# Another list of orders and engines for 1571 operations of an attention and feed-forward kernel

## The chip, the cores and the metric

The kernel runs on one core of a Trainium2 chip. The metric is the time of one execution on the device in microseconds (us); of the runs before the change the median is 259.77 us (three runs, 259.72 to 259.9). TensorE (PE in the rows) multiplies matrices, VectorE (DVE), ScalarE (ACT) and GpSimd (POOL) do the elementwise work, SyncE (SP) only starts transfers. GpSimd and ScalarE start some transfers as well.

## The reference

A Nystrom attention with 32 landmarks over 8 batches of 8 heads, 576 rows and 64 columns, then a feed-forward layer with a residual on its output (8 x 576 rows of 512):

```python
q_lm = q.reshape(B, H, m, S // m, D).mean(axis=3)          # m = 32 landmarks
k_lm = k.reshape(B, H, m, S // m, D).mean(axis=3)
A = sm(q, k_lm); Bm = sm(q_lm, k_lm); C = sm(q_lm, k)      # sm: softmax of a b^T / sqrt(D)
Z = Bm.transpose(0, 1, 3, 2) / (norm1(Bm) * norminf(Bm) + 1e-06)
for _ in range(6):
    Z = 2 * Z - Z @ Bm @ Z
x = A @ Z @ C @ v                                          # heads side by side: (8, 576, 512)
xn = (x - mean(x)) / sqrt(var(x) + 1e-06) * g_ln
out = x + relu(xn @ w_ch1) @ w_ch2                         # w_ch1 512 x 2048, w_ch2 2048 x 512
```

`norm1` and `norminf` stand for the two matrix norms; the sums and means are over each head or row.

## The kernel before, in words

**The stages of one batch.** q and k of a batch are loaded and cast to 16 bits (`nat_q`, `nat_k`; two units of four heads each). Sums over the 18 rows of a segment give the landmarks (for batch 1 the products `psl_q` and `psl_k`, with `pairs16`). A product of landmarks (`psb`), its softmax, and six steps of the iteration give Z: a step is a few matmuls on tiles of 32 rows into the tile `it` (`it<-st`), after which VectorE makes the next state `st` from it (`next_`, L210). The steps alternate between the two engines, and another step can't begin before that state is there. Batch 1 alone forms set 1, batches 2 and 3 set 2, 4 and 5 set 3, 6 and 7 set 4; batch 0 has its own code (`def_batch0`, L531). C v (`product`, `cv`) and Z are multiplied into `zt` (TensorE's `pszt`, then a copy) and into `zc`, from which VectorE makes `zsum` and `zcbd`. The numerator of A is `ea`, scaled by its row sums (`psd`, a logarithm and an exponential on ScalarE, `norm` on GpSimd or VectorE).

**The feed-forward layer.** W1 comes in eight loads through a staging buffer (`stg`, six buffers that q, k and v of batch 0 use first) and is scaled by g_ln in sixteen operations (`scale_w1`, L352 to L357) on GpSimd, ScalarE or VectorE. W2 comes in four loads on GpSimd's queue, straight into place. Because x = ea^T zcbd, the first layer is taken as ea^T (zt W1): four products `psm` per batch, on tiles of 64 rows and 32 columns, then a copy `m` (for batches 0 and 1 with the correction `less` for the mean, made of `psf`, a sum of four matmuls over W1), and then 16 chunks `psh`, each followed by a relu on ScalarE (L203) or VectorE (L1068) into `hT`. The second layer is `pso` = hT^T W2 by blocks of 128 rows (batches 0 and 1, in pairs of matmuls) or, from batch 2 on, seven products of half-size blocks (`ps7a`, `ps7c`, `ps7e`) with sums of parts of hT (`hmix`) and of W2 (`mix`) in front of them. The rows x themselves are `psy`; `done` and `add7` on VectorE add the second layer to them, and two stores per block (`store`, on SyncE, ScalarE or GpSimd) write 128 KB each.

**What sets the order.** Every operation is registered with its name, the engines that may do it, the buffers that it uses and a function (`op`, L158). The table `ORDER` (from L19) lists all 1571 of them by number, with a letter for the engine: P TensorE, D VectorE, A ScalarE, G GpSimd, S SyncE. The loop at the end of the program goes through it:

```python
    for n, e in order:
        emit(n, e)
```

`emit` (L174) takes a buffer for a name at its first use, in the order of the list, and gives it back behind the last use; `keep` (L188) fixes that each engine works through its instructions in that order. So the list sets three things: the order on each engine, the engine of each operation that may go to several, and which buffer a load has to wait for. There are two PSUM buffers of two banks (`p2`) and four of one bank (`bank`). At the start 80 matmuls on zeros (`idle`, the operations `warm`) keep TensorE busy while the first loads are under way; these too have their places in the list.

## Time and profile before

| | |
|---|---|
| median of the runs | 259.77 us (259.72 to 259.9) |
| the profiled execution | 260.21 us |
| its span | 258.5 us |
| TensorE busy | 249.3 us, 96% of the span, 3499 matmuls |
| VectorE busy | 212.1 us, 82%, 472 instructions |
| ScalarE busy | 164.0 us, 63%, 304 instructions |
| GpSimd busy | 177.6 us, 69%, 180 instructions |
| moved by DMA | 36.32 MB, mean 140 GB/s |

The span reaches from the first to the last instruction that the profiler recorded; the execution's time is 1.71 us longer than it. A busy share is taken over the whole span. A row of the timeline gives the start and the length of a run of equal instructions on one engine in us, the engine, the line of the program, the operation, the tile written and the tiles read, the shape, how many instructions there are (x8), and in brackets how long the engine stood idle before it and what ended that. TensorE's rows overlap by the time that a matmul needs to drain, so the time between two starts says what a group costs, not its length. "L193" is the helper through which every matmul goes, so groups are told apart by their tiles.

### The profile page before, as it was taken

The numbers are of one execution on the slowest core, as the hardware profiler recorded it, in microseconds if no ns is written. First come the engines' busy times: TensorE is split into PE (matmuls) and PEld (weight loads), VectorE is DVE, ScalarE is ACT, GpSimd is POOL, SyncE is SP. The second block draws the span as 40 slices with busy tenths as digits, with TensorE's granted clock in tenths as the row PEclk, the third lists the DMA queues.
The fourth block names the chain that finished last, engine by engine and source line by source line (L and its number), as shares of the span: only waits on it lengthen the run. The fifth ranks groups of instructions, "written<-read, shape, count | busy, mean of one in ns | idle before, by whom it ended". The sixth has DMA issues, their size and how long they took to land.

```text
span 258.5 us, 8352 instructions
## 1 busy us (share of the span) xinstructions
PE 249.3 (96%) x3499; PEld 178.4 (69%) x3499; DVE 212.1 (82%) x472; ACT 164.0 (63%) x304; POOL 177.6 (69%) x180
## 2 busy tenths in 40 slices
PE   7689999999999999999999999999999999999994
PEld 7566565555654457777776787777867787788882
DVE  1669899999999989996998879887537999878761
ACT  1588886737766899778756996878766246544000
POOL 8324899689893789699999996782068505966600
PEclk9999999999999999999999999999999999999998
DMA  6999999999749275949814832400130100500356
GB/s 236 364 281 341 365 207 202 207 230 258 230 121 161 44 160 80 207 100 279 144 21 111 235 96 63 114 16 3 41 85 0 44 20 3 122 22 14 90 120 185
DMA packets 23278, 36.32 MB, mean 140 GB/s; under 512 B 2117, under 2 KB 11593, under 8 KB 23241
## 3 DMA queue, kind: packets, MB, share of 16 engines
q1 hardware_dynamic: 12376, 23.34, 29.9%
q0 software_dynamic: 9504, 10.36, 25.3%
q10 hardware_dynamic: 1360, 2.10, 3.2%
q8 instruction: 27, 0.44, 0.7%
q14 instruction: 11, 0.08, 0.1%
HBM read 36.70 MB, written 9.44 MB: 178 GB/s over the span
## 4 chain that ended last, share of the span: by engine, by line
PE 88%; DMA 6%; ACT 2%; DVE 1%; issue 0%; POOL 0%; ACTq 0%; POOLq 0%
PE psh L193 24%; PE ps7a L193 16%; PE pso L193 15%; PE ps7c L193 8%; DMA nat_q<-in_q_dram 5%; PE ps7e L193 4%; PE psm L193 4%; PE psy L193 3%; PE it L193 3%; PE psec L193 2%; PE pscv L193 2%; DMA stg_k<-in_k_dram 2%; PE psd L193 1%; PE psea L193 1%; PE psf L193 1%; PE pso_74a L193 1%
## 5 line engine op out<-in xcount | busy, mean ns | idle before, releaser
L203 ACT ACTIVATE hT<-psh 128x576 f16<-128x576 f32 x106 | 65.8, 650 | 30.4 <-PE psh L193 28.6
L193 PEld LDWEIGHTS <-hT 128*128 128x128 f16 x688 | 64.4, 98 | 23.3 <-issue 3.7
L193 PE MATMUL psh<-ea,m 128*128 128x288 f16 x512 | 78.3, 287 | 0.1
L193 PEld LDWEIGHTS <-m 128*128 128x128 f16 x512 | 48.8, 98 | 15.7 <-issue 1.3
L193 PE MATMUL pso<-w,hT 128*128 128x512 f16 x176 | 45.7, 380 | 0.1
L207 POOL TENSOR_TENSOR mix<-hT 128x1024 f16<-128x1024 f16 x8 | 17.0, 2128 | 27.4 <-ACT hT L203 27.4
L210 DVE SCALAR_TENSOR_TENSOR x<-ps7a,rstd,x 128x256 f32<-128x256 f32 x48 | 21.3, 476 | 6.2 <-PE ps7a L193 4.4
L193 PE MATMUL ps7a<-mix,hT 128*128 128x256 f16 x192 | 25.6, 273 | 0.0
L1068 DVE TENSOR_SCALAR hT<-psh 128x576 f16<-128x576 f32 x22 | 16.4, 753 | 10.1 <-PE psh L193 9.9
L997 DVE BATCH_NORM_STATS2 six<-x 128x6 f32<-128x512 f32 x36 | 24.2, 673 | 0.0
L207 POOL TENSOR_TENSOR ea<-ea,lns 128x576 f16<-128x576 f16 (+1 forms) x14 | 17.7, 1261 | 8.0 <-ACT lns L203 4.3
L200 ACT CAST m<-psm 128x512 f16<-128x512 f32 (+1 forms) x25 | 19.1, 792 | 4.5 <-PE psm L193 3.4
L200 ACT COPY x<-psy 128x512 f32<-128x512 f32 (+1 forms) x29 | 16.8, 587 | 7.7 <-PE psy L193 7.3
L193 PEld LDWEIGHTS <-mix 128*128 128x128 f16 x192 | 18.3, 98 | 4.3 <-issue 1.5
L207 POOL TENSOR_TENSOR mix<-mix,hT 128x1024 f16<-128x1024 f16 x8 | 17.0, 2127 | 6.2 <-DVE mix L207 5.8
L207 POOL TENSOR_TENSOR hT<-hT 128x1024 f16<-128x1024 f16 x9 | 19.1, 2123 | 0.2
L207 POOL TENSOR_TENSOR hT<-hT,mix 128x1024 f16<-128x1024 f16 x7 | 15.1, 2169 | 4.4 <-PE ps7e L193 2.5
L214 DVE TENSOR_REDUCE part<-xT_k 128x32 f16<-128x576 f16 x24 | 17.1, 736 | 0.0
L207 POOL TENSOR_TENSOR asum_q<-asum_q 128x256 f32<-128x256 f32 (+1 forms) x24 | 15.1, 629 | 1.5
L203 ACT ACTIVATE ec<-psec 128x256 f16<-128x256 f32 (+1 forms) x42 | 12.4, 431 | 5.3 <-PE psec L193 5.3
L193 PE MATMUL psy<-zcbd,ea 128*128 128x256 f16 x80 | 14.8, 273 | 0.2 <-ACT x L200 0.2
L357 POOL TENSOR_SCALAR w<-w1s,g_sb 128x512 f16<-128x512 f32 x12 | 8.2, 693 | 9.4 <-DMA w1s<-in_moe_w_ch_dram 5.5
(174 smaller groups left out, 473.1 us busy)
## 6 DMA issues: line engine op xcount, KB each, us to landing
out_dram<-x SPq DMA_DIRECT2D x55, 128.0 KB, 2.6
stg_v<-in_v_dram SPq DMA_DIRECT2D x10, 576.0 KB, 5.9
w1s<-in_moe_w_ch_dram SPq DMA_DIRECT2D x8, 512.0 KB, 11.6
nat_q<-in_q_dram POOLq DMA_DIRECT2D x7, 576.0 KB, 8.3
nat_k<-in_k_dram POOLq DMA_DIRECT2D x7, 576.0 KB, 8.2
w<-in_moe_w_ch_dram POOLq DMA_DIRECT2D x4, 512.0 KB, 9.0
out_dram<-x ACTq DMA_DIRECT2D x15, 128.0 KB, 2.4
stg_v<-in_v_dram SPq DMA_DIRECT2D x6, 288.0 KB, 4.3
```

The lines of the kernel that those rows point to most:

```text
L193: keep(nc.tensor.matmul(o, l, r, start=start, stop=stop, tile_position=(rb, cb), skip_group_check=(skip or cb != 0)))
L200: keep(nc.scalar.copy(o, i) if e == "A" else ENGINES[e].tensor_copy(out=o, in_=i))
L203: keep(nc.scalar.activation(*args, **kw))
L207: keep(ENGINES[e].tensor_tensor(out=o, in0=a, in1=b, op=f))
L210: keep(ENGINES[e].scalar_tensor_tensor(out=o, in0=a, scalar=s, in1=b, op0=f0, op1=f1))
L214: keep(nc.vector.tensor_reduce(out=o, in_=i, axis=axis, op=f))
L357: keep(ENGINES[e].tensor_scalar(out=o, in0=src, scalar1=g_sb[:, kk:kk + 1], scalar2=0.0, op0=ALU.mult, op1=ALU.add))
L997: keep(nc.vector.bn_stats(out=T(f"six_{j}")[:], in_=T(f"x_{j}")[:]))
L1068: keep(nc.vector.tensor_scalar(out=o, in0=T(psh)[:, :, 0:HS], scalar1=0.0, scalar2=None, op0=ALU.max))
```

## The change

Only the table `ORDER` is exchanged; no other line differs. Both lists hold the same 1571 operations, and TensorE has 622 of them in both. Its first rows:

```diff
-0G 20P 23P 4S 12P 14P 24P 17P 11P 2S 1S 3S 6S 7S 10P 21P 28G 38P 25A 26D 34P 39D 40P 29P 30A 31P 27D
...
+0G 21P 4S 18P 12P 23P 22P 14P 2S 24P 20P 17P 11P 10P 1S 25D 3S 13P 28G 40P 38P 39D 6S 26A 34P 27D 7S
...
```

Of operations that may go to several engines these change theirs: of the relus 18 go from VectorE to ScalarE and 6 back; of the stores 19 go from SyncE to ScalarE, 10 from ScalarE to SyncE and 2 to GpSimd; of the sums of parts of hT (`hmix`) 11 go from VectorE to GpSimd and 10 back; of the copies `m` 8 go from ScalarE to VectorE and 6 back; of the copies `x` 7 go from ScalarE to VectorE and 5 back; of the operations `norm` 4 go from VectorE to GpSimd and 3 back; a few casts and scalings move too. By operations, VectorE has 398 before and 388 now, ScalarE 312 and 331, GpSimd 153 and 154, SyncE 86 and 76.

**Batch 0's iteration on TensorE.** `it` holds the products of its steps, a new `st` marks a new step; `psl_q` reads q of batch 1, `psf` reads W1, `psd` belongs to `ea`, and `pszt` is the product behind the last step. LDWEIGHTS loads the operand that stays in the array. Before, from the fourth step on:

```order
L193 MATMUL it_366<-st_578 32x64
...
L193 MATMUL it_366<-st_593 32x64
...
L193 MATMUL psd_603<-ea_572,bones_75 128x288
...
L193 MATMUL psl_q_608<-nat_q_427,pairs16_68 128x128
...
L193 MATMUL idle_622<-zeros_63 128x128
...
L193 MATMUL it_366<-st_620 32x32
...
L193 MATMUL pszt_643<-st_641,cv_618 32x32
...
L193 MATMUL psf_677<-w1_16_78,lesser_74 128x512
```

Now, from the second step on:

```order
L193 MATMUL it_407<-st_556 32x64
...
L193 MATMUL it_407<-st_575 32x64
...
L193 MATMUL psl_q_592<-nat_q_473,pairs16_68 128x128
...
L193 MATMUL it_407<-st_590 32x64
...
L193 MATMUL psf_617<-w1_16_78,lesser_74 128x512
...
L193 MATMUL it_407<-st_613 32x64
...
L193 MATMUL psd_630<-ea_579,bones_75 128x288
...
L193 MATMUL it_407<-st_634 32x32
...
L193 MATMUL psf_617<-w1_16_78,lesser_74 128x512
...
L193 MATMUL pszt_652<-st_644,cv_577 32x32
```

The first nine `psl_q` matmuls stood behind the fifth step and `psd`, with fillers behind them; now they stand behind the third step. Two matmuls of the first `psf`, which stood behind `pszt`, now stand between the steps.

**The same place on VectorE**, from the last states of the iteration to the first two `m`. `w_16_78<-w1s` is a scaling of W1, `cv` and `zt` and `zcbd` are as above, and `xT_q<-nat_q` and `lmt_q` belong to batch 1. Before:

```order
L210 SCALAR_TENSOR_TENSOR st<-st,it 128x128
L633 TENSOR_SCALAR cv<-pscv,rcv,cinv 128x130
L210 SCALAR_TENSOR_TENSOR st<-st,it 128x2x32
L220 STREAM_TRANSPOSE xT_q<-nat_q 128x576
L200 CAST zt<-pszt 128x2x32
L214 TENSOR_REDUCE zsum<-pszc 128x2
L200 CAST zt<-pszt 128x2x32
L220 STREAM_TRANSPOSE lmt_q<-tot_q 128x64
L207 TENSOR_TENSOR zcbd<-pszc,heads_71 128x256 x2
L207 TENSOR_TENSOR ea<-ea,lns 128x288
L210 SCALAR_TENSOR_TENSOR m<-less,zsum,psm 128x512 x2
```

Now:

```order
L633 TENSOR_SCALAR cv<-pscv,rcv,cinv 128x130
L210 SCALAR_TENSOR_TENSOR st<-st,it 128x128
L210 SCALAR_TENSOR_TENSOR st<-st,it 128x2x32
L357 TENSOR_SCALAR w_16_78<-w1s,g_sb 128x512
L214 TENSOR_REDUCE zsum<-pszc 128x2
L207 TENSOR_TENSOR zcbd<-pszc,heads_71 128x256 x2
L200 CAST zt<-pszt 128x2x32
L220 STREAM_TRANSPOSE xT_q<-nat_q 128x576
L210 SCALAR_TENSOR_TENSOR m<-less,zsum,psm 128x512 x2
```

A scaling of W1 is new on VectorE behind the last state, the transpose of q has gone behind the copy of `zt`, the other copy of `zt` has gone to ScalarE, and the transpose to `lmt_q` and the product of `ea` no longer stand ahead of the `m`.

**The iteration of set 3 on TensorE** (`it` and `st` with other numbers), with the `psm` of batch 3. Before:

```order
L193 MATMUL psh_2847<-ea_2193,m_2676 128x288
L193 LDWEIGHTS zt_2129
L193 MATMUL psm_2852<-w1_16_78,zt_2129 32x512
...
L193 MATMUL psm_2867<-w1_16_78,zt_2129 32x512
L193 LDWEIGHTS st_2820
L193 MATMUL it_2739<-st_2820 32x64
...
L193 MATMUL psy_2937<-zcbd_2150,ea_2193 128x256
...
L193 MATMUL it_2739<-st_2894 32x64
```

Now:

```order
L193 MATMUL ps7a_2414<-mix_1723,hT_2264 128x256
...
L193 MATMUL it_2696<-st_2757 32x64
...
L193 MATMUL psm_2893<-w1_16_78,zt_2126 32x512
...
L193 MATMUL psm_2904<-w1_16_78,zt_2126 32x512
...
L193 MATMUL it_2696<-st_2916 32x64
```

The two `psm`, which stood between `psh` and the first step, now stand between the first step and the second, where products of 128 rows stood. On GpSimd the four loads of W2 move too: behind the first of them, where a load of q and four scalings of W1 stood ahead of the second load, one scaling stands now, and the load of q comes behind both.

168 lines of the change are left out of this document (84 added, 84 removed).

## The prediction, made before the changed kernel was run

> **What bounds the kernel now.** I read the page first, then the four stretches of the span, then what TensorE waited for, and last the rows of the first 43 us.
>
> ```profile
> span 258.5 us, 8352 instructions
> PE 249.3 (96%) x3499; PEld 178.4 (69%) x3499; DVE 212.1 (82%) x472; ACT 164.0 (63%) x304; POOL 177.6 (69%) x180
> ...
> PE 88%; DMA 6%; ACT 2%; DVE 1%; issue 0%; POOL 0%; ACTq 0%; POOLq 0%
> ```
>
> TensorE is busy 96% of the span and holds 88% of the chain that ended last. The same 3499 matmuls run after the change, so the time can move only where TensorE stands idle or loses time between matmuls. Where that is, the stretches show (busy time and instructions of PE, PEld, DVE, ACT and POOL, then granted clock, DMA share, GB/s):
>
> ```profile
> 0.00:20.30 20.30, 15.87 (x344) 13.23 (x344) 10.16 (x35) 10.93 (x16) 9.14 (x33) 1.00 0.97 292
> 20.30:42.47 22.17, 21.48 (x326) 12.84 (x308) 20.81 (x51) 18.08 (x39) 17.98 (x25) 1.00 1.14 289
> 42.47:254.65 212.18, 211.94 (x2849) 152.37 (x2848) 180.75 (x387) 134.97 (x250) 150.51 (x124) 1.00 0.50 111
> ```
>
> From 42.47 to 254.65 TensorE is idle 0.24 us: nothing is to be had there but the small losses between kinds of matmul. The first 20.30 us hold 4.43 us of idle time beside the filler matmuls on zeros, with the DMA engines full (share 0.97); what follows 254.65 is the last addition and its store. In the view of waits one of TensorE's is put down to a DMA, 0.21 us for q of batch 1 (in brackets at 18.73 below). No matmul waits for W2 or for q and k of batch 2 in this execution, so an order that bears their lateness has nothing to win here by that alone.
>
> **The change part by part.** *The start.* The rows of TensorE that carry batch 0's iteration (its steps are `it<-st`):
>
> ```profile
> 16.61 0.24 PE L193 MATMUL it<-st 32*32 32x64 f16 x8
> ...
> 17.29 0.24 PE L193 MATMUL it<-st 32*32 32x64 f16 x8
> 17.92 0.24 PE L193 MATMUL it<-st 32*32 32x64 f16 x8 [0.40 <-DVE st L210]
> ...
> 18.73 0.66 PE L193 MATMUL psl_q<-nat_q,pairs 128*128 128x128 f16 x9 [0.21 <-DMA nat_q<-in_q_dram]
> 19.22 0.39 PE L193 MATMUL idle<-zeros 128*128 128x128 f16 x4
> 19.54 0.22 PE L193 MATMUL it<-st 32*32 32x32 f16 x8
> 20.09 0.21 PE L193 MATMUL pszt<-st,cv 32*32 32x32 f16 x8 [0.33 <-DVE st L210]
> ...
> 21.32 0.76 PE L193 MATMUL psm<-w,zt 64*32 64x512 f16 x8
> ...
> 23.73 1.14 PE L193 MATMUL psh<-ea,m 128*128 128x288 f16 x8
> ```
>
> `psl_q` starts when q of batch 1 lands, at about 18.7 us. It stood behind the fifth step (17.92); now it stands behind the third (16.61), so steps four to six come after the landing. GpSimd issues that load at the same place of its list, and the DMA engines were full, so I take the same landing. Then step four starts at 18.73 + 0.49 (`psl_q`'s 18.73 to 19.22) = 19.22. A round of the iteration is 0.63 (17.29 to 17.92), so step six starts at 20.48, and `pszt` 0.55 later (19.54 to 20.09) at 21.03: 0.95 us later than 20.09. Two of the four `psf` that follow are now done inside those rounds; a third waits for a W1 piece that VectorE now scales between the last step and the zsum, zcbd and zt copies. VectorE has no such row. The same operation on GpSimd is 693 ns, and VectorE casts 1152 elements from fp32 in 0.76, so 512 of them are 0.34:
>
> ```profile
> L357 POOL TENSOR_SCALAR w<-w1s,g_sb 128x512 f16<-128x512 f32 x12 | 8.2, 693 | 9.4 <-DMA w1s<-in_moe_w_ch_dram 5.5
> ...
> 6.51 0.76 DVE L200 CAST nat_k<-stg_k 128x1152 f16<-128x1152 f32 x1 [3.37 <-DMA stg_k<-in_k_dram]
> ...
> 19.96 0.77 DVE L220 STREAM_TRANSPOSE xT_q<-nat_q 128x576 uint32<-128x576 uint32 x1
> ...
> 22.24 1.40 DVE L210 SCALAR_TENSOR_TENSOR m<-less,zsum,psm 128x512 f16<-128x512 f16 x2
> ```
>
> I take 0.5. It stands where the 0.77 transpose of q at 19.96 stood; that transpose goes behind the zt copy, ahead of the two `m` (1.40 together), while an `ea` product and a transpose that stood there no longer do, and one zt copy is now ScalarE's. So VectorE has about as much to do between `pszt` and the `m` as before, `psm` starts 0.95 later, near 22.3, and `psh` at about 24.7 where it started at 23.73: **+1.0 us**. Bounds: +0.8 and +1.2 by the two prices of the scaling; and -0.3 if q has landed by 17.2, when the steps run through and half a round of waiting (0.63) is saved.
>
> *From there to batch 1's `psm` (42.47).* Here before lost time that a later TensorE gets back:
>
> ```profile
> 27.95 0.72 ACT L203 ACTIVATE w<-w1s,g_sb 128x512 f16<-128x512 f32 x1 [0.75 <-DMA w1s<-in_moe_w_ch_dram]
> 28.58 0.56 ACT L200 CAST less<-psf 128x512 f16<-128x512 f32 x1
> ...
> 29.20 1.04 PE L193 MATMUL psf<-w,lesser 128*128 128x512 f16 x4
> 30.17 0.88 PE L193 MATMUL psm<-w,zt 64*32 64x512 f16 x8
> ```
>
> The `psf` at 29.20 waited for ScalarE's `less` (to 29.14), which stood behind a scaling that waited for W1 until 27.95: about 0.3 lost. The `psm` at 30.17 is spread over 0.8 (the next `psh` starts at 30.98) where an undisturbed one takes 0.35 (below): 0.45 lost to the `m` before it. Now that scaling is VectorE's, and TensorE comes a microsecond later to both: 0.75 back. Against it, the first relus of batch 0 are ScalarE's, and six exponentials `ec` stand on it before the next two relus: I take 0.15 lost. Sum **-0.6**; bounds -0.9 (smaller waits to 42 regained) and 0 (new ones eat it).
>
> *The kinds of matmul.* Products on 32- and 64-row tiles cost something each time TensorE goes from full-array matmuls to them and back:
>
> ```profile
> 60.80 1.15 PE L193 MATMUL psh<-ea,m 128*128 128x288 f16 x8
> 61.87 0.41 PE L193 MATMUL psm<-w,zt 64*32 64x512 f16 x8
> 62.22 1.04 PE L193 MATMUL pso<-w,hT 128*128 128x512 f16 x4
> ...
> 94.58 0.65 PE L193 MATMUL psh<-ea,m 128*128 128x288 f16 x4
> 95.16 0.63 PE L193 MATMUL psm<-w,zt 64*32 64x512 f16 x16
> 95.72 1.04 PE L193 MATMUL pso<-w,hT 128*128 128x512 f16 x4
> ```
>
> One `psm` takes 0.35 to the next full matmul (61.87 to 62.22), two back to back 0.56 (95.16 to 95.72), so joining two saves 0.14 at the exit. At the entry, eight `psh` matmuls and the switch took 1.07 (60.80 to 61.87), four and the switch 0.58 (94.58 to 95.16); four more cost 0.49, so the switch cost 0.09. Together 0.23, of which I take 0.2 for each group saved. Counted in the two lists from batch 1's first `psm` on, small-tile products stand in 45 groups before and 40 now: **-1.0 us**; bounds -1.15 (0.23 each) and -0.5 (half lost again).
>
> *Where groups grew tight.* In set 3 a step, two `psm` and the next step now form one group, in set 4 a step, a `psec` and the next step. Between two steps VectorE must make the next state:
>
> ```profile
> 119.67 0.29 PE L193 MATMUL it<-st 32*32 32x64 f16 x16
> ...
> 120.03 0.42 DVE L210 SCALAR_TENSOR_TENSOR st<-st,it 128x256 f16<-128x256 f16 x1
> ```
>
> From the step's start to the end of the state is 0.78 (119.67 to 120.45). Two `psm` cover 0.56 of it, which leaves 0.22; a `psec`, of like size, I give the same: 0.44, with the hand-over to TensorE **+0.5**; bounds 0 (the step itself covers as much) and 0.9 (VectorE late by a relief of 0.2 each).
>
> *What costs nothing.* Eighteen relus go from VectorE to ScalarE and six back; by the groups of the page
>
> ```profile
> L203 ACT ACTIVATE hT<-psh 128x576 f16<-128x576 f32 x106 | 65.8, 650 | 30.4 <-PE psh L193 28.6
> ...
> L1068 DVE TENSOR_SCALAR hT<-psh 128x576 f16<-128x576 f32 x22 | 16.4, 753 | 10.1 <-PE psh L193 9.9
> ```
>
> VectorE is relieved by 12 x 0.753 = 9.0 us and ScalarE loaded by 12 x 0.65 = 7.8, both still under TensorE's 249.3, which covers them; without that cover a relu costs its 0.65 where `psh` follows `psh`. Stores move to ScalarE's queue among its relus:
>
> ```profile
> 66.51 0.57 ACTq L223 DMA_DIRECT2D out_dram<-x  x1
> 66.53 0.66 ACT L203 ACTIVATE hT<-psh 128x576 f16<-128x576 f32 x1
> ```
>
> The relu behind a store starts with its issue, and each moved store's block is added long before: nothing. The last three stores stay as they were; two of the blocks before go to GpSimd, which has nothing left behind them: 0, at worst the 0.81 that a load's issue takes there (row of 28.65 below).
>
> The sum is +1.0 - 0.6 - 1.0 + 0.5 = -0.1. The profiled execution took 260.21 (span 258.5 and 1.71 around it), 0.44 above the median of 259.77; with -0.1 it would be 260.1, and the median of the runs **259.7**.
>
> **The rivals.** *Start free* (faster): q of batch 1 lands early. The first W1 load now takes another buffer of the staging pool, that of q's first half, so it may be queued later and leave the DMA engines to q, k and v. The start then gives -0.3 and the next stretch nothing: -0.3 - 1.0 + 0.5 = -0.8, 259.0. Against it: the W1 load stood behind v on the same queue anyway.
>
> *W2 waited for* (slower): the third pair of `pso` matmuls of block 0, on the second W2 piece, stood behind the steps of set 1 and now stands between the fourth and the fifth of them; the fifth began at 39.33, so with the later start I put the pair near 40:
>
> ```profile
> 39.33 0.20 PE L193 MATMUL it<-st,ident 128*128 128x64 f16 x1
> ...
> 28.65 0.81 POOL L223 DMA_DIRECT2D w<-in_moe_w_ch_dram  x1
> ...
> w<-in_moe_w_ch_dram POOLq DMA_DIRECT2D x4, 512.0 KB, 9.0
> ```
>
> The piece is now issued one scaling behind the first, 28.65 + 0.81 + 0.69 = 30.2, and lands at 39.2 by the median of 9.0. It is waited for from a landing at 40 on: with two more microseconds in the queue, 41.2, TensorE stands 1.2 with everything behind that pair: -0.1 + 1.2 = +1.1, and 259.77 + 1.1 = 260.9. For it: the DMA share of 1.14 in the second stretch. Against it: the median of 9.0.
>
> *The clock falls* (slower): fillers on zeros that stood between batch 0's products go ahead of them, and TensorE stands idle from about 16.9 (the third step's 16.61 and 0.24) to 18.7. Matmuls of 128 columns ran 2.96 us for 28 at the beginning (0.106 each), and 30 fillers in 1.89 after it; at the first rate 1.8 us of products behind the pause would take 3.0 to 3.6:
>
> ```profile
> 1.40:4.36 2.96, 2.96 (x28) 1.00 0.74 223
> 4.36:6.25 1.89, 1.89 (x30) 1.00 1.04 411
> ```
>
> 0.106 against 0.063 (1.89 / 30) is a factor of 1.7, though the granted clock reads 1.00 in both: at most +1.8 with all of it lost, 261.5. The Trainium skill, "TensorE: Matmul & The Clock Gate", section "Part 1: The HAM clock gate", speaks for a fall only after an idle window of about 3.4 us and counts such windows freely of the kernel. By that rule a pause of 1.8 us keeps the clock, and the start's +1.0 stands as it is; no row here shows a fall.
>
> **How the numbers follow.** A time within 0.2% (0.52 us) of 259.77 is about what a measurement cannot tell from no change. The forecast, 259.7 with its own range 259.1 to 260.3, gets 0.47: 0.10 faster, 0.31 same, 0.06 slower. Start free gets 0.28, with the small waits regained too: 0.26 faster, 0.02 same. W2 waited for, or the upper bounds of the start, gets 0.20, slower. The clock gets 0.05, slower. Together 0.36, 0.33 and 0.31. The range reaches to the sum of -0.3, -1.0 and no tight groups (258.4) and to 260.9 with a little of the clock: 258.4 to 261.0.
>
> **What would show it.** Right: `psl_q` at 18.7 with an idle time of over 1 us before it, `pszt` near 21.0, the first `psh` near 24.7, batch 1's `psm` near 44 with three `pso` pairs ahead of it that stood behind, and from there to the last matmul 0.5 us less for the same work. Wrong: a `psl_q` before 18, a wait of `pso` for `w`, matmuls of 128 columns at 0.106 after 10 us, or over 1 us of idle TensorE after 45 us. If later stretches hold waits that the old order did not have, the term for groups fails first.

## The result, and the profile after

The changed kernel takes **261.86 us** (median of four, 261.55 to 262.23) where the kernel before took 259.79 in the same comparison: a ratio of 1.008, interval 1.0062 to 1.0097, or 2.07 us slower. That lies above the predicted range, which ended at 261.0. (Comparisons leave disturbed executions out, so a ratio can differ a little from that of two medians.) The profiled execution took 261.55, with a span of 259.8, so 1.75 lie around it; against the profiled execution before that is 1.34 more.

The head of the page, its slices of the granted clock, and its chain:

```profile
span 259.8 us, 8340 instructions
PE 251.6 (97%) x3499; PEld 180.0 (69%) x3499; DVE 209.6 (81%) x462; ACT 167.9 (65%) x315; POOL 179.8 (69%) x181
...
PEclk9995999999999999999999999999999999999998
...
PE 88%; DMA 6%; DVE 2%; ACT 1%; POOL 0%; issue 0%; POOLq 0%
```

TensorE is busy 2.3 us longer with the same 3499 matmuls, and one slice of the clock reads 5. The same four stretches as before (columns as there):

```profile
0.00:20.30 20.30, 16.74 (x322) 14.02 (x322) 10.16 (x33) 8.80 (x14) 8.76 (x33) 0.97 0.96 289
20.30:42.47 22.17, 21.87 (x299) 12.96 (x299) 20.18 (x48) 17.21 (x37) 19.07 (x23) 0.87 1.14 292
42.47:254.65 212.18, 212.18 (x2870) 152.46 (x2869) 178.34 (x383) 141.87 (x265) 151.93 (x126) 1.00 0.50 109
254.65:259.80 5.15, 0.78 (x14) 0.61 (x11) 0.90 (x2) 0.00 (x0) 0.00 (x0) 0.85 0.51 152
```

At 42.47 TensorE has started 621 matmuls where it had started 670. The clock is 0.87 in the second stretch. Finer, for TensorE alone (busy time and matmuls, granted clock, DMA share, GB/s):

```profile
12.46:15.87 3.41, 2.73 (x84) 1.00 1.10 263
15.87:19.28 3.41, 2.16 (x51) 1.00 1.13 283
19.28:22.70 3.42, 3.41 (x48) 0.50 1.12 298
22.70:26.11 3.41, 3.41 (x26) 0.50 1.05 399
```

The trace has the clock at half for 6.83 us, from 19.28 to 26.11, which is two windows of 3.41 (e1's expectation below has it 0.36 too late). What TensorE did around it:

```profile
17.06 0.24 PE L193 MATMUL it<-st 32*32 32x64 f16 x8 [0.40 <-DVE st L210]
17.87 0.66 PE L193 MATMUL psl_q<-nat_q,pairs 128*128 128x128 f16 x9 [0.58 <-DMA nat_q<-in_q_dram]
18.46 0.24 PE L193 MATMUL it<-st 32*32 32x64 f16 x8
...
20.57 0.41 PE L193 MATMUL pszt<-st,cv 32*32 32x32 f16 x16
...
22.66 0.77 PE L193 MATMUL psm<-w,zt 64*32 64x512 f16 x8
23.37 1.14 PE L193 MATMUL psl_q<-nat_q,pairs 128*128 128x128 f16 x9
...
25.67 1.36 PE L193 MATMUL psh<-ea,m 128*128 128x288 f16 x8
```

Nine `psl_q` take 0.66 at 17.87 and 1.14 at 23.37. The first `psh` starts at 25.67 instead of 23.73. The end of TensorE's work, before and after:

```profile
253.57 1.06 PE L193 MATMUL pso_74b<-w,hT 128*128 128x128 f16 x16
```

```profile
254.38 1.06 PE L193 MATMUL pso_74b<-w,hT 128*128 128x128 f16 x16
```

So of 1.3 us in the span, 0.81 are there when the last products start, and 0.5 come behind them. To split this further I took, for each two successive matmuls, the time between their starts beyond the median of two of the same kind before, and summed it: time lost up to batch 1's first `psm` (42.47 before, 45.13 after; three pairs of `pso` moved ahead of it, which this measure takes account of), from there to the last matmul, and then the time from the start of the last matmul to the end of the span.

| kernel | lost up to batch 1's `psm` | lost behind it | last matmul to end | span |
|---|---|---|---|---|
| before | 9.61 | 25.16 | 4.09 | 258.5 |
| changed | 10.97 | 24.60 | 4.62 | 259.8 |

That is +1.36, -0.56 and +0.53: the start is what cost, the long middle gained, and the end cost again.

### The profile page after: what moved, and what is told of

It reads as the page before. It is cut to its first block, busy times and chain, and to the rows that moved or that the text cites. A ratio compares the mean times of both kernels' runs of the same rounds, so it can differ in the third digit from the quotient of the medians.

```text
span 259.8 us, 8340 instructions
## 1 busy us (share of the span) xinstructions
PE 251.6 (97%) x3499; PEld 180.0 (69%) x3499; DVE 209.6 (81%) x462; ACT 167.9 (65%) x315; POOL 179.8 (69%) x181
## 4 chain that ended last, share of the span: by engine, by line
PE 88%; DMA 6%; DVE 2%; ACT 1%; POOL 0%; issue 0%; POOLq 0%
PE psh L193 24%; PE ps7a L193 16%; PE pso L193 15%; PE ps7c L193 8%; DMA nat_q<-in_q_dram 5%; PE ps7e L193 4%; PE psy L193 4%; PE psm L193 4%; PE it L193 3%; PE psd L193 2%; PE pscv L193 2%; DMA stg_k<-in_k_dram 2%; PE psec L193 1%; PE psea L193 1%; PE pso_74a L193 1%; PE psf L193 1%
## 5 line engine op out<-in xcount | busy, mean ns | idle before, releaser
L203 ACT ACTIVATE hT<-psh 128x576 f16<-128x576 f32 x118 | 74.0, 652 | 32.6 <-PE psh L193 28.7
L193 PE MATMUL psh<-ea,m 128*128 128x288 f16 x512 | 79.2, 287 | 0.0
L207 POOL TENSOR_TENSOR mix<-hT 128x1024 f16<-128x1024 f16 x10 | 21.2, 2126 | 34.1 <-ACT hT L203 19.3
L200 ACT CAST m<-psm 128x512 f16<-128x512 f32 (+1 forms) x23 | 17.1, 779 | 3.2 <-PE psm L193 3.1
L207 POOL TENSOR_TENSOR hT<-hT,mix 128x1024 f16<-128x1024 f16 x8 | 17.3, 2167 | 2.2 <-DVE mix L207 2.2
L207 POOL TENSOR_TENSOR hT<-hT 128x1024 f16<-128x1024 f16 x8 | 18.1, 2258 | 0.2
L200 ACT COPY x<-psy 128x512 f32<-128x512 f32 (+1 forms) x27 | 15.8, 591 | 3.6 <-PE psy L193 3.5
L207 POOL TENSOR_TENSOR mix<-mix,hT 128x1024 f16<-128x1024 f16 x7 | 14.8, 2125 | 0.4
L207 POOL TENSOR_TENSOR asum_q<-nat_q 128x512 f32<-128x512 f16 x12 | 14.1, 1172 | 0.7 <-DMA nat_q<-in_q_dram 0.3
L203 ACT ACTIVATE lns<-psd 128x576 f32<-128x576 f32 x16 | 10.4, 651 | 5.4 <-PE psd L193 4.9
```

The costliest lines, as they stand in the source:

```text
L193: keep(nc.tensor.matmul(o, l, r, start=start, stop=stop, tile_position=(rb, cb), skip_group_check=(skip or cb != 0)))
L200: keep(nc.scalar.copy(o, i) if e == "A" else ENGINES[e].tensor_copy(out=o, in_=i))
L203: keep(nc.scalar.activation(*args, **kw))
L207: keep(ENGINES[e].tensor_tensor(out=o, in0=a, in1=b, op=f))
```

## The experiments

Seventeen kernels were run, each beside the kernel before on the same chip. The column on the clock counts the executions whose mean granted clock is below 0.9945. 6.83 us at half, in a span of 260, take away 0.013, one window of 3.41 half of that. The other executions read 0.995 to 1.000; in the profiles what is missing there lies behind the last matmul (0.85 in the last stretch above). Of the kernel before, 6 of 127 executions in these comparisons are below.

| run | median us (executions) | before | ratio, interval | clock fell in |
|---|---|---|---|---|
| changed | 261.86 (4) | 259.79 | 1.008, 1.0062 to 1.0097 | 4 of 4 |
| e1 fillers between the steps | 260.74 (12) | 260.05 | 1.0032, 1.0002 to 1.0063 | 2 of 12 |
| e2 before, its fillers ahead | 260.19 (11) | 260.05 | 1.0015, 0.9996 to 1.0035 | 5 of 11 |
| e3 q behind step five | 261.78 (9) | 260.05 | 1.0057, 1.0034 to 1.008 | 4 of 9 |
| e4 end much as before | 262.63 (6) | 260.05 | 1.0101, 1.0071 to 1.0131 | 6 of 6 |
| e5 start before, rest changed | 261.27 (14) | 260.24 | 1.0028, 1.0006 to 1.0049 | 5 of 14 |
| e6 start changed, rest before | 266.17 (6) | 260.24 | 1.0201, 1.0155 to 1.0248 | 5 of 6 |
| e7 fillers, v load early | 263.66 (6) | 260.24 | 1.0128, 1.009 to 1.0166 | 3 of 6 |
| e8 the same, q behind step five | 264.46 (6) | 260.24 | 1.014, 1.0098 to 1.0182 | 4 of 6 |
| e9 fillers, cast of v later | 260.79 (12) | 259.94 | 1.0043, 1.0025 to 1.0061 | 2 of 12 |
| e10 start before, rest changed, cast later | 260.71 (12) | 259.94 | 1.0028, 1.0013 to 1.0043 | 0 of 12 |
| e11 q behind, fillers, cast later | 261.16 (11) | 259.94 | 1.0034, 1.0013 to 1.0054 | 2 of 11 |
| e12 one filler | 262.11 (6) | 259.94 | 1.0062, 1.0038 to 1.0085 | 3 of 6 |
| e13 as e9, end as before | 261.14 (10) | 260.17 | 1.0042, 1.0026 to 1.0057 | 1 of 10 |
| e14 before, changed end | 260.6 (11) | 260.17 | 1.0011, 1.0002 to 1.0019 | 0 of 11 |
| e15 all mended, end as before | 261.44 (7) | 260.17 | 1.0053, 1.003 to 1.0077 | 2 of 7 |
| e16 all mended, own end | 260.47 (12) | 260.1 | 1.0039, 1.0013 to 1.0066 | 4 of 12 |
| e17 as e16, seven fillers | 260.48 (12) | 259.92 | 1.0023, 1.0006 to 1.004 | 0 of 12 |

In the edits below an operation stands by its name instead of its number; `warm` is a filler of four matmuls on zeros, `total_q11` is the first nine `psl_q`.

### The clock: e1, e2, e12

Theory: the half clock, brought on by fillers that went to the front, is what the changed list lost. Rival: three steps stand behind q's landing, and the half clock is hidden.

```diff
e1, against the changed list
- warm_14 warm_10 warm_7 warm_1 warm_0 load_q00 cast_q00 load_q01 warm_3 cast_k01
+ warm_14 warm_0 load_q00 cast_q00 load_q01 cast_k01
- step_0_0 next_0_0 psa_1 step_0_1 next_0_1 ... step_0_2 next_0_2 total_q11
+ step_0_0 warm_3 next_0_0 psa_1 step_0_1 warm_1 next_0_1 ... step_0_2 warm_7 warm_10 next_0_2 total_q11
```

> The changed kernel with four of its filler operations (16 matmuls on zeros) taken from the block at the start and put between the steps of batch 0's iteration: one behind the first step, one behind the second, two behind the third, ahead of psl_q. Nothing else moves. Clock theory: in the changed kernel TensorE's clock is granted at half from 19.64 to 26.47 us because the stretch before it was too empty; with the gaps filled it stays at 1.00 (mean 0.997 instead of 0.984), TensorE comes to batch 1's first psm 1.3 to 2 us earlier, and the time is 260.0 to 260.6. Rival, the order around q: what is lost is lost because three steps stand behind the landing of q, and half clock is hidden behind VectorE and the W1 loads: the clock is 1.00, but the time stays within 0.4 of 261.86.

The median came to 260.74, 0.69 above the kernel before where the changed list was 2.07 above. In the stretch of the half clock the profile now shows

```profile
16.23:19.64 3.41, 3.22 (x72) 1.00 1.14 284
19.64:23.05 3.41, 2.78 (x48) 1.00 1.08 315
23.05:26.47 3.42, 3.29 (x41) 1.00 1.06 406
```

the clock full, and the last products start at 253.66 instead of 254.38. So some 1.4 us of the loss, read from the two distances to the kernel before, went with 16 filler matmuls at another place (e1's interval alone reaches from 0.05 to 1.6 us). The two profiles lie 1.20 apart at batch 1's `psm` (45.13 and 43.93) and 0.72 at the last products; the 0.5 between is a wait of `psh` behind a cast on ScalarE, 0.60 in e1 and 0.10 in the changed kernel, of which more below. The median is a little outside the band (260.0 to 260.6) on the high side; a rest of 0.7 stays. The rival, which wanted the time within 0.4 of 261.86, is out.

```diff
e2, against the list before
- ... warm_0 ... warm_8 psb_0 ... gram_b_0 warm_12 warm_9 warm_5 ... turns_q1 warm_3 ... total_q11 ... warm_6
+ ... warm_0 warm_12 warm_9 warm_5 warm_3 warm_6 warm_8 ... psb_0 ... gram_b_0 ... turns_q1 ... total_q11 ...
```

> The kernel before with its six late filler operations (24 matmuls on zeros, which stood between the products of batch 0 from psb on) moved into the block at the start; nothing else moves. Clock theory: the clock falls to half for about 6.8 us somewhere between 12 and 23 us, mean clock near 0.98, and the time is 260.8 to 261.8. Rival, the order around q: fillers produce nothing and the products keep their order, so the time stays at 259.8, within 0.3.

The clock fell in 5 of 11 executions instead of in next to none. Two of those took 260.15 and 260.34, hardly more than the 260.07 that the six others have as their median, two took 261.82 and 261.94, and the profiled one, with three windows at half, 263.69. So executions with a fall lie from 0.1 to 3.6 us above the others' median here. The median over all, 260.19, lies in neither band. The theory had expected a fall every time, and 1 us or more for it. What holds is that the clock falls more often without these fillers: the emptied start is about an even chance.

```diff
e12, against the changed list
- warm_3 ... step_0_2 next_0_2 total_q11
+ step_0_2 warm_3 next_0_2 total_q11
```

> The changed kernel with one filler operation (4 matmuls on zeros, 0.2 us) taken from the start and put behind the third step, ahead of psl_q. Clock theory with a threshold on how full a stretch of 3.4 us is: the changed kernel's stretch before the fall holds 0.29 of the array's time, this makes it about 0.35, between that and the least of the kernel before (0.39), so the clock falls in some of the runs and not in others; runs with it at 0.98 are 1 us or more above those at 1.00. Rival, only an idle stretch counts: one filler does not alter that TensorE is never idle for more than 0.6 us, and the clock falls in all runs as in the changed kernel.

As the theory had it: 3 of 6. The three that fell took 262.08 to 262.21, the others 260.85 to 262.13. The profiled one fell for one window, which here begins elsewhere in the program:

```profile
19.75:23.17 3.42, 2.49 (x40) 1.00 1.08 326
23.17:26.58 3.41, 3.41 (x26) 0.50 1.05 403
```

Counted over the runs with the changed start: with no filler behind the first steps the clock fell in 10 of 10 executions (the changed list and e4; 15 of 16 with e6), with one in 3 of 6 (e12), with four in 13 of 64 (e1, e9, e11, e13, e15 and e16, below), and with seven in 0 of 12 (e17). The place of `psl_q` counts too: behind the fifth step the clock fell in 4 of 9 with no filler (e3), in 8 of 30 with four (e11, e15, e16), and e17's seven are of that order; behind the third it is 5 of 34 with four (e1, e9, e13). The mean clock does not tell where in the span a fall lay. Some follow a wait for a transfer instead: e7 and e8, also with four fillers, fell in 3 and 4 of 6, and in e7's profile the clock is at half from 51.98 on, behind a wait of 2.0 us for W2. In e5 (start of before) TensorE waits 3.0 us, and the windows read

```profile
67.00:70.42 3.42, 0.38 (x16) 1.00 0.69 207
70.42:73.83 3.41, 3.41 (x10) 0.50 0.71 217
```

These are near to what the Trainium skill names in "TensorE: Matmul & The Clock Gate", "Part 1: The HAM clock gate", a window in which TensorE idles, though neither wait is as long as a window of 3.41.

### Where q stands: e3

```diff
e3, against the changed list
- step_0_2 next_0_2 total_q11 scale_w1_20 tot_q11 step_0_3 ... step_0_4 cv_00 load_w1_4 psd_01
+ step_0_2 next_0_2 scale_w1_20 step_0_3 ... step_0_4 cv_00 load_w1_4 psd_01 total_q11 tot_q11
```

> The changed kernel with the first nine psl_q (and the copy of their result) put back behind the fifth step and psd, as they stood before; the fillers stay at the start. Rival, the order around q: steps four to six no longer wait for q, zt is ready some 0.9 us earlier, and the time is 260.7 to 261.1. Clock theory: the same matmuls fall into the same stretch, the clock falls all the same, and the time is 261.4 to 262.0.

The time, 261.78, is in the clock theory's band, but not by the clock: it fell in 4 of 9, and the five others have a median of 261.61. The profile, of an execution at full clock, says that both theories had a point. At 46 us this TensorE had lost 0.85 less than the kernel before: putting q behind the fifth step is worth about what the prediction charged for the reverse. Then it stood 2.6 us in one place; the longest waits of TensorE and the row of ScalarE that it waited behind:

```profile
PE psh L193 <- ACT hT L203: 2.6, 1, 2.6
...
67.37 1.17 ACT L200 CAST natv<-stg_v 128x1152 f16<-128x1152 f32 x1 [2.56 <-DMA stg_v<-in_v_dram]
68.44 1.18 ACT L203 ACTIVATE hT<-psh 128x576 f16<-128x576 f32 x2
```

ScalarE casts half of batch 2's v ahead of two relus, and the load landed late. In the changed kernel's own profile that cast starts at 66.98, a few hundredths behind its landing, and waits for nothing, since TensorE and the relus come later there.

### The halves: e5 and e6

e5 takes the first 264 entries of the list before and then what is left in the order of the changed list; e6 the other way round, with 266.

> The first 264 entries of the list before (to ahead of batch 1's first psm, near 42 us), and the rest in the order and on the engines of the changed list. Theory that the whole loss lies in the start: no half clock, and the rest is worth what the prediction's later terms gave or less: 259.2 to 259.8 (the kernel before on this chip 260.0). Rival, the late v load: in the changed list ScalarE casts v of batch 2's second half, whose load stands behind two stores on SyncE's queue and lands just in time; a start that is earlier than the changed one only waits there, and the time is 260.3 to 261.5, with a wider spread than the kernel before.

> The first 266 entries of the changed list (to ahead of batch 1's first psm), and the rest as before. Clock theory: the clock falls to half for 3.4 to 6.8 us in most runs, TensorE comes to the rest about 1 us late, and the time is 260.9 to 261.9. Theory that the rest of the changed list is what is slow: 259.8 to 260.3.

e5 is 0.28% slower (0.7 us) and spreads from 260.38 to 265.85. Its profiled execution waits 3.0 us at the same cast. So the theory that all lies in the start is out: with the start of before, the rest of the changed list still loses. e6 fell in clock 5 of 6 times, but its 266.17 is far above both bands: TensorE waits 1.6 us for a `psm` and 1.0 for a `psh` on VectorE's work behind the seam. The two halves do not fit there, and e6 says nothing on its question.

### The load of v: e7 to e10

```diff
e7, against e1
- store_3_0 load_v31 ... store_0_1 ... load_v21
+ load_v31 ... load_v21 store_3_0 store_0_1
```

> The changed kernel with the four fillers between the steps (as in the first experiment) and, on SyncE's queue, the load of v's second half of batch 2 ahead of the two stores that stood before it. Late-v theory: ScalarE's wait for that load and TensorE's 0.4 us of psh behind it go, and the time is 0.4 to 0.9 below the first experiment, 259.8 to 260.3, with a smaller spread. Rival: the load lands at the same time because the queues of transfers are full, and the time stays at 260.7 within 0.2.

> As the run before, with psl_q also put back behind the fifth step and one filler each behind steps one to four. In the profile of the third experiment TensorE was 0.85 us further at 46 us than in the kernel before, and lost it, and more, waiting for v. If that wait was all that took it back, the time is 259.0 to 259.5, below the kernel before. If something later takes it back, it is 259.8 to 260.5.

Both failed, e7 with 263.66 and e8 with 264.46. TensorE's longest wait in e7 is

```profile
PE pso L193 <- DMA w<-in_moe_w_ch_dram: 2.5, 2, 2.0
```

for W2, which nothing in the changed profile waited for. The first of the two stores had been a gate: SyncE waits in it until batch 0's block is done, near 55 us. Without it both loads of v started at 36 to 39 us, and W2's third and fourth pieces landed at 51.4 and 54.0 instead of 46.8 and 49.5. e9 and e10 leave SyncE alone and move only the cast:

```diff
e9, against e1 (and e10, against e5)
- expb_2 ... cast_v21 relu_113 relu_112
+ expb_2 ... relu_113 relu_112 cast_v21
```

> The changed kernel with the four fillers between the steps, and on ScalarE the cast of v's second half of batch 2 two places later, behind the two relus that stood behind it; no load moves. Late-v theory: the relus no longer stand behind a load that lands just in time, TensorE's wait for ScalarE's hT near 67 us goes, and the time is 0 to 0.3 above the kernel before of the same runs (the first experiment was 0.83 above). Rival: the remainder lies in the later order, not in this wait, and the time stays 0.6 to 1.0 above the kernel before.

> The start of the kernel before (264 entries), the rest of the changed list, and the same cast two places later. The run without that move was 0.73 above the kernel before and its TensorE waited 3.0 us in one place for ScalarE behind that cast. Late-v theory: 0 to 0.3 above the kernel before of the same runs, and no wait of psh for hT over 0.5 us. Rival, as above: 0.6 to 1.0 above.

That wait is gone from both profiles, and so are the executions of 265 us: e10 spreads from 260.44 to 261.65. But both medians stay where they were, 0.85 and 0.77 above the kernel before; the rival's band was 0.6 to 1.0. This does not clear the cast, for the move brought a wait of its own. Behind the two relus the cast, 1.17 us on ScalarE, holds up a copy and a relu after it, and TensorE waits for that relu (e1, then e9):

```profile
68.03 0.65 PE L193 MATMUL psh<-ea,m 128*128 128x288 f16 x4 [0.43 <-ACT hT L203]
```

```profile
69.96 0.69 PE L193 MATMUL psec<-xT_k,lm 32*32 32x288 f16 x28 [0.30 <-ACT hT L203]
```

By the time between starts, as in the table above, TensorE loses 0.60 at the first and 0.58 at the second; the second is 0.62 in e10 and 0.59 in e11, e13 and e15 to e17, which all keep the cast there. In the kernel before GpSimd does this cast, and no such wait stands there. No run gives the cast alone back to GpSimd, so what it costs as a whole is not settled. The last products of e9 start level with the kernel before (253.57), and its span is still 0.4 longer:

```profile
253.59 1.06 PE L193 MATMUL pso_74b<-w,hT 128*128 128x128 f16 x16
...
core 0: 258.9 us, clock 1.000
```

### The end: e4, e14, e13

```diff
e4, against the changed list
- seven_73_04 pso_74a_00 ... pso_74a_02 ... seven_76_14 ... store_32_0:S ... store_34_0:G add7_760 store_33_1:G
+ seven_73_04 ... seven_76_14 store_31_0 store_31_1 add7_751 store_32_0 store_32_1 add7_760 add7_761 store_33_1:S store_34_1:A store_34_0:A store_33_0 pso_74a_00 pso_74a_02
```

> The changed kernel with the end as it was before: the first two pairs of pso_74a go back behind the last of the seven products, the last additions and stores ahead of pso_74a, and two stores return from GpSimd to ScalarE and SyncE. From the last matmul to the end of the span the changed kernel takes 4.59 us, the one before 4.09. Theory that the tail cost this: the time is 0.4 to 0.7 below 261.86. Rival: the last stores wait for the queue of transfers whatever their place, and the time stays within 0.2.

The clock fell in all six (fillers as in the changed list), and the time did not come down: it is 0.77 above 261.86, outside both bands. In its profile the span ends 4.47 behind the last matmul, against 4.62, and TensorE lost 0.3 more in its last products, which the two pairs of `pso_74a` had covered. e14 asks the question from the other side, without the clock: the list before up to entry 1460, then the changed one.

> The list before up to its entry 1460, and the last 111 operations as in the changed list. Theory of the crowded end: the last matmul starts where it did, within 0.3 us, the span ends 4.5 to 4.6 us after it instead of 4.1, and the time is 0.3 to 0.6 above the kernel before. Rival: within 0.2 of it.

0.11% (0.3 us; by the medians 0.43) above the kernel before. The last products start where they did, and the span ends later:

```profile
253.53 1.06 PE L193 MATMUL pso_74b<-w,hT 128*128 128x128 f16 x16
...
core 0: 258.7 us, clock 1.000
```

That is 4.30 behind the last matmul instead of 4.09, less than the 4.5 to 4.6 expected. The stores from 249 us on, of the kernel before and of the changed one (KB each, median us to landing):

```profile
out_dram<-x ACTq DMA_DIRECT2D x5, 128.0 KB, 2.9
out_dram<-x SPq DMA_DIRECT2D x4, 128.0 KB, 2.5
```

```profile
out_dram<-x ACTq DMA_DIRECT2D x3, 128.0 KB, 2.9
out_dram<-x SPq DMA_DIRECT2D x3, 128.0 KB, 2.8
out_dram<-x POOLq DMA_DIRECT2D x2, 128.0 KB, 3.5
```

With the changed list the last 12 stores are issued within 4.5 us, behind 6 us without one; before, the last 13 are issued within 5.1 us, and three more in the 3 us ahead of those. The very last takes 2.85 us to land, before 2.17. Whether it is the crowd or GpSimd's two slower issues (3.5 us) isn't told apart; e4, which took GpSimd's away, gained 0.15 (4.62 to 4.47). e13 put the old end on e9:

> The ninth run's kernel (the changed list with fillers between the steps and the cast later) up to its entry 1460, and the last 111 operations in the order and on the engines of the list before. Theory of the crowded end: in every kernel with the changed end 12 stores are issued within 4.5 us of the last one, the last takes 2.85 us to land instead of 2.17, and the span ends 4.5 to 4.6 us after the last matmul instead of 4.1. Then it ends 4.1 us after it here, and the time is 0.3 to 0.6 below the ninth run's 0.85 above the kernel before: 0.2 to 0.6 above. Rival: the end does not matter beyond 0.1, since TensorE's last products decide; the time stays 0.7 to 1.0 above.

Its span ends 4.06 behind the last matmul, as expected, but the graft brought a new wait, so the time says nothing:

```profile
241.60 1.48 PE L193 MATMUL ps7a<-mix 128*128 128x256 f16 x12 [0.42 <-DVE mix L207]
```

### All of it together: e11, e15, e16, e17

> The changed kernel with psl_q behind the fifth step, one filler each behind steps one to four, and the cast two places later; the order of SyncE is that of the changed list. If the clock and the v load are all that the changed list loses, the 0.85 us by which psl_q behind the fifth step was further at 46 us stays, and the time is 0.3 to 0.9 below the kernel before of the same runs. If transfers decide from there on, it is within 0.3 of it.

Above the kernel before by 0.34%, outside both bands. Its executions lie between 259.9 and 262.0, and the profiled one shows the prediction's W2 rival at work, the third pair of `pso` of block 0 ahead of the fifth step:

```profile
40.20 0.59 PE L193 MATMUL pso<-w,hT 128*128 128x512 f16 x2 [0.70 <-DMA w<-in_moe_w_ch_dram]
```

e15 moves that pair behind the sixth step (and two pairs of block 1 ahead), and takes the old end; e16 keeps the changed end; e17 adds three fillers.

```diff
e16, against e11
- pso_00_02 pso_00_04 ... step_1_4 ... pso_01_00 ... step_1_5 ... pso_01_02
+ pso_00_02 ... pso_01_00 step_1_4 ... pso_01_02 step_1_5 pso_00_04
e17, against e16
- warm_13 warm_12 warm_4 ...
+ gram_a_0 warm_13 ... turn_g warm_4 warm_12
```

> The changed list with psl_q behind the fifth step, one filler behind each of steps one to four, the cast of v later, the third pair of pso (which waited 0.7 us for W2's second piece in the eleventh run) behind the last step of set 1 with two pairs of block 1 in its place, and the last 111 operations as before. If the clock, the v load, W2's second piece and the crowded end are what the changed list loses, the time is 0.2 to 0.8 below the kernel before of the same runs; if transfers that land late find another place to wait, 0 to 0.8 above.

> As the fifteenth run (psl_q behind the fifth step, a filler behind each of steps one to four, the cast of v later, the third pair of pso later), but with the changed list's own end, so that the wait of 0.42 us for a sum of hT that the grafted end brought is gone. In the fifteenth run TensorE stood 0.3 us ahead of the kernel before at 240 us. If that holds and the crowded end costs its 0.4, the time is within 0.3 of the kernel before of the same runs. If W2's second piece or v lands later than in that profile, 0.3 to 1.0 above.

> As the sixteenth run, with three more filler operations (12 matmuls on zeros) taken from the start: two ahead of the product with v, which waited 0.73 us there, and one behind the products for the scaling of Z. In the sixteenth run the clock fell in 4 of 12 executions, and those took 1.7 to 3 us more than the others, which were level with the kernel before. Clock theory: with the stretches fuller the clock falls in at most 1 of 12, and the time is 0.4 below to 0.2 above the kernel before of the same runs. Rival: the slow executions are those in which transfers land late, and the clock falls because TensorE then waits; they stay as frequent, and the time is 0.3 to 1.0 above.

e15 carries e13's graft wait with it, waits another 0.5 for W2 near 47 us, and is 0.53% slower, outside both bands. The eight executions of e16 without a fall have a median of 260.16, level with the 260.1 of the kernel before; the four with one have 262.46. Its profile, one without, is the furthest of all on TensorE:

```profile
252.73 1.06 PE L193 MATMUL pso_74b<-w,hT 128*128 128x128 f16 x16
...
core 0: 258.2 us, clock 0.997
```

In e17 the clock fell in none of 12 and the upper end came down from 263.23 to 262.01, which fits the fall as the cause of those slow executions; e16 and e17 ran on different chips, so it isn't settled. And the median is 0.23% (0.6 us) above the kernel before, in the rival's band; three more fillers have their price too, or transfers land late in other ways. That stays open. No version beat the kernel before, and each from e9 on that keeps the changed middle also keeps the cast on ScalarE, with its 0.6.

| kernel | lost up to batch 1's `psm` | lost behind it | last matmul to end | span |
|---|---|---|---|---|
| before | 9.61 | 25.16 | 4.09 | 258.5 |
| e9 | 9.70 | 25.09 | 4.52 | 258.9 |
| e10 | 9.55 | 25.42 | 4.49 | 259.1 |
| e14 | 9.64 | 25.09 | 4.30 | 258.7 |
| e16 | 8.82 | 25.11 | 4.59 | 258.2 |

## Why the prediction was wrong, point by point

**The step that failed is the rival on the clock**, which got 0.05. Its place (the pause ahead of `psl_q`), its cause (the fillers that went to the front), and nearly its price (+1.8, 261.5) were there. What was wrong was the reason for the small chance: that the clock falls only after a long pause. TensorE's longest pause ahead of the fall is 0.58, and in the window before it was busy 2.16 of 3.41 us. Two of the prediction's own signs of being wrong came with it: `psl_q` starts before 18, at 17.87, and matmuls of 128 columns run at 0.103 after 10 us (nine from 23.37 to 24.30). In the kernel before, two windows of the same stretch read

```profile
7.77:11.18 3.41, 2.03 (x47) 1.00 1.06 389
...
14.60:18.01 3.41, 2.93 (x98) 1.00 1.12 279
```

and the first of them, with less busy time (2.03 of 3.41), had no fall behind it, so busy time alone doesn't decide either. What goes with the falls is how much of the array the matmuls use: `psl_q` (9 x 128 columns), `psd` and `psf` on all 128 x 128, but the steps on a sixteenth of it and `psa` on an eighth. Columns at full rate (512 in 0.216 us), weighted by that share, come to 0.29 of the window from 15.87 to 19.28, against 0.40 or more in the windows of the kernel before.

All the profiles bear this out. Each trace's changes of clock are whole multiples of 3.41 us apart, so its windows can be counted from them. In the 19 profiles there are 1374 windows at full clock up to the last matmul. Eight were followed by a fall, with a use of 0.07 to 0.34, those of e5 and e7 (0.07 and 0.33) among them; none of the other 1366 has less than 0.35. Busy time and pauses do not part them: a window of e3 busy for 1.57 us, with a pause of 1.84, has a use of 0.52 and no fall, and the one ahead of e12's fall is busy for 2.49, with no pause over 0.56, at 0.27. The first window at full clock begins between 4.07 and 6.68 us, so an empty stretch can lie in one window or across two, which fits that one list falls in some executions and not in others. The limit was found after the fact, on one execution of each kernel; that it is array use and not something that goes along with it isn't shown. The Trainium skill, "TensorE: Matmul & The Clock Gate", section "Part 1: The HAM clock gate", which I had let decide, names an idle window as what brings the lower clock; here none was idle; the falls of e5 and e7 come nearer to it. Its window length agrees: 6.83 us are two of 3.41.

**The start's +1.0** was right where the clock was not at half. In e9, where it is full, the rows are

```profile
18.50 0.68 PE L193 MATMUL psl_q<-nat_q,pairs 128*128 128x128 f16 x9 [0.69 <-DMA nat_q<-in_q_dram]
20.93 0.43 PE L193 MATMUL pszt<-st,cv 32*32 32x32 f16 x16
22.90 0.41 PE L193 MATMUL psm<-w,zt 64*32 64x512 f16 x8
...
24.70 1.23 PE L193 MATMUL psh<-ea,m 128*128 128x288 f16 x8
```

for 18.7, 21.03, 22.3 and 24.7 in the forecast; batch 1's `psm` stands at 43.85, forecast near 44. The small waits then gave back more than 0.6: up to that `psm` e9 has lost 0.09 more than the kernel before, forecast +0.4. In the changed kernel q landed at 17.83, so `pszt` came at 20.57, earlier than forecast; what made `psh` 25.67 was the clock. By this 1.27 of the 1.36 lost in the start are the clock's (1.36 - 0.09); the two profiles are from different chips.

**The kinds of matmul, -1.0, and the tight groups, +0.5.** Neither was right, and their sum was. The measure of lost time, from batch 1's first `psm` on, by kind of transition:

| | before | changed |
|---|---|---|
| into groups of small tiles | 3.93 | 3.75 |
| out of them (46 times; 41 now) | 8.82 | 8.40 |
| between unlike small kinds inside a group | 1.97 | 2.53 |
| inside one small kind | 9.04 | 8.96 |
| between full-array matmuls | 1.40 | 0.95 |

Five exits fewer saved 0.18 and 0.42 at the edges, and 0.56 of it went into transitions inside the joined groups: joining a `psm` to a step saves almost nothing, since leaving a `psm` costs about 0.31 whatever comes next. My 0.2 per group came from two `psm` joined to each other. And the tight place in set 3 waits for nothing:

```profile
121.58 0.29 PE L193 MATMUL it<-st 32*32 32x64 f16 x16
121.85 0.63 PE L193 MATMUL psm<-w,zt 64*32 64x512 f16 x16
122.42 0.30 PE L193 MATMUL it<-st 32*32 32x64 f16 x16
```

From step to step is 0.84, the 0.78 that the state needs plus the hand-over, with the `psm` at their usual 0.57 in between: the step's own time had to be counted to the cover, as the term's lower bound had it. The gain of 0.56 behind batch 1's `psm`, forecast 0.5, is mostly the last line: two small waits of the kernel before, 0.28 at 84.0 and 0.26 at 143.1, have no counterpart. They have none in e9 and e16 either, so TensorE's lateness is not what covered them. That e9 gains only 0.07 there, and e10 loses 0.26, is mostly the wait of 0.58 and 0.62 behind the cast. So the sum was right by luck.

**What costs nothing.** This held the work moved to ScalarE against TensorE's 249.3 us and counted no wait. The cast of v that went from GpSimd to ScalarE makes TensorE lose 0.5 to 0.6 at 67 to 69 us in e1, e4, e9 and e12, and 0.10 in the changed kernel's profile, which is the fastest of its four executions. The share of a whole span does not say whether an engine is free where it is needed.

**Stores and the end, 0.** This missed 0.5 (4.09 to 4.62). The forecast looked at what the issue of a store holds up on its engine and not at when the data of the last blocks are ready: with two pairs of `pso_74a` ahead of the last products of seven, the last crowd of stores begins 3.8 us ahead of the last matmul (12 stores) instead of 4.5 (13). The very last is issued 0.64 behind that matmul in both and takes 0.68 longer to land.

**The rivals.** *Start free* didn't come. *W2 waited for* didn't come in the changed kernel, which was late at that place by its clock, but came as described in e11 (a landing at 40.2, a wait of 0.7) and in e7 and e8 for the later pieces.

**What is settled and what is not.** Of 2.07 us about 1.3 are the clock: 1.27 in the profile, some 1.4 by e1. About 0.4 are the end (0.2 to 0.5 in the profiles, 0.3 to 0.43 in e14). The profiles account for 1.34 in all; what the times have beyond that fits the wait behind the cast of v, which other executions have and the profiled one hardly, against a gain of about 0.65 that the new order has in the middle without it. No run isolates either.

## What to carry to other kernels

A filler matmul has two jobs, and the second is easily lost when an order is searched by start times: it keeps the stretch full enough for the clock. Where a list moves fillers ahead of small-tile products, count the array's use over a few microseconds, not only TensorE's pauses. A store that waits in a queue can be what holds the loads behind it back from transfers that are needed first, so a load is not free to go earlier only because its buffer is. A cast or a relu moved to an engine with idle time to spare can still hold up what stands behind it: look at the place, not at the share. And a gain at the start is not simply a gain to add: e1 won 1.20 us at batch 1's `psm` and kept 0.72 of it, since a wait behind it grew.

## What the runs showed of the hardware that I had not expected

The clock fell to half with TensorE busy two thirds of the time, for one, two or three windows of 3.41 us, and not in every execution: the same kernel fell in 3 of 6 or 5 of 11. By the measure of array use it fell behind windows of 0.34 or less. At half clock, where the measure cannot much exceed 0.5, it stayed down behind five windows of 0.37 or less and came back behind eight of 0.43 or more. Two windows at half cost the changed kernel about 1.3 us; e16's executions with a fall, of whatever length, have a median 2.3 us above the others.

An elementwise sum on VectorE took 2.34 us in e15 while GpSimd worked on such sums, and 0.69 in the kernel before, where it began as GpSimd had just ended (VectorE and GpSimd in e15, then the same in the kernel before):

```profile
237.95 2.34 DVE L207 TENSOR_TENSOR mix<-hT 128x1024 f16<-128x1024 f16 x1
...
237.63 2.12 POOL L207 TENSOR_TENSOR hT<-hT 128x1024 f16<-128x1024 f16 x1
```

```profile
238.57 0.69 DVE L207 TENSOR_TENSOR mix<-hT 128x1024 f16<-128x1024 f16 x1
...
236.16 2.13 POOL L207 TENSOR_TENSOR hT<-hT 128x1024 f16<-128x1024 f16 x1
```

In the kernel before, a relu on VectorE ahead of the sum had put it there. In e15 VectorE's sum ends at 240.29; GpSimd's ended at 239.75, and 0.69 later is 240.44, so it did most of its work once GpSimd was done. The Trainium skill, "SBUF — State Buffer", section "SBUF: two separate sides", has the two engines lock each other out of a shared pair of ports for a whole instruction, and these rows agree but for the 0.15 us. The graft's wait of 0.42 was for a sum behind this one, which it made late by up to its 1.65 us more.
